# Where the row-maximum pieces of an attention stage stand between its score tiles: the second piece of a phase moved from the opening to the end

## The chip, the cores and the metric

The kernel runs on one core of a Trainium2 chip. The metric is device time in microseconds for one launch. Five engines work side by side and wait for each other by semaphores: TensorE (PE, with its weight loads shown apart as PEld), VectorE (DVE), ScalarE (ACT), GpSimd (POOL) and SyncE (SP, which issues the DMAs). Each takes its own instructions in the order in which the program lists them.

## The reference

An attention layer whose queries are pooled in pairs, followed by two MLP blocks that mix over the sequence and over the channels. Only the attention is touched here.

```python
batch, n_heads, seq, head_dim = (4, 8, 1152, 64)
q_pool = q.reshape(B, H, S // factor, factor, D).mean(axis=3)      # factor = 2: 576 queries
scores = scale * np.matmul(q_pool, k.transpose(0, 1, 3, 2))
scores = scores - np.max(scores, axis=-1, keepdims=True)
attn = np.exp(scores)
attn = attn / (np.sum(attn, axis=-1, keepdims=True) + 1e-09)
attn_out = np.matmul(attn, v)
# then _moe_ref (w_in, w_spatial, w_out) and _moe2_ref (U, V, w_ch1, w_ch2) on [4, 576, 512]
```

## The kernel before

The 32 heads are taken as 16 pairs, one head on partitions 0 to 63 and the other on 64 to 127. For a pair the scores are 576 queries by 1152 keys for each head; they are computed transposed (keys on partitions), since the second product needs them so. The row maxima that are subtracted must be known before the exponential, so they come from a separate pass with rounded operands, one pair ahead.

That pass is cut into 11 *pieces* a pair, 176 in all (`pieces`, `piece`). A piece is a few matmuls into a PSUM tile `r` and a maximum over that tile on DVE. There are three forms. The common one has two matmuls of 512 columns side by side (L169) and a reduce over 1024 columns (L191). The full-array one has two matmuls of 512 columns one after the other (L186, L187). The rest piece has four or six matmuls of 128 columns (L169, L199; L202), and when it is the second rest piece of a pair four small reduces follow it (L211, L214); every rest piece ends with L215. When all pieces of a pair are there, `to_rows` transposes the maxima on PE (L230, L237) and ACT copies them into a row (L240, L247).

The main loop runs over 108 *groups* `i` of four key chunks of 128, each chunk with 192 queries; 27 groups make four pairs. A group is two *score tiles* `s`: eight matmuls with q and k (L256), two that subtract the row of maxima (L272), then one exponential of 128x768 on ACT (L279). POOL adds the results up for the denominators (L297, L286, L300). After every odd group PE does the second product, `po` (L307), for the two groups before it, and, where a query third is complete, the sums (L321). So two groups, an even one and an odd one, make a *phase*: opening, two score tiles, a middle, two score tiles, an end, then a block of `po` matmuls. There are 54 phases.

Pieces may stand at the opening, in the middle and at the end. How many is set by `end`, which asks for a number of finished pieces that grows by 11 in 6.75 groups, and by `some(beside, lag)`, which puts one piece if fewer than `end - lag` are done. Before the change, an even group's opening puts one piece and then, with `lag=1`, possibly a second; the middle and the end put one each. The first five groups follow a table of their own (`FIRST`).

Score tiles, pieces and the transposed maxima all take their PSUM from one ring, `ps_s`, of three slots of two banks each. A new tile takes the slot that was given out three tiles earlier, and its first matmul waits until the last reader of that tile is through: the DVE reduce if it was a piece, the ACT exponential if it was a score tile.

Between the groups `also(i)` advances the preparation of the MLP weights: casts on ACT (L583, L584, L664), bit operations on DVE (L588, L590, L594), sums on POOL (L592, L669). The casts of the next pair's k and q (`round_k` L149, `round_q` L138 and L143) stand on ACT too, between the exponentials of two groups. On DVE the reciprocals of the sums (L329, two halves) and the product that makes an output tile (`out`, L335) stand among the reduces.

Of the kernel before, what the change touches and what calls it, by code (L numbers as in the profile page):

```python
# [30 lines left out]
FIRST = (11, 12, 15, 18, 21)  # L31
# [4 lines left out]
def attention(tc, idf, q, k, v, xs, rounded, also):  # L36
# [14 lines left out]
    NP, D, _, _, T = q.shape  # L51
    S = k.shape[3]
    HP = NP // len(xs)
    KC = S // 128
# [13 lines left out]
    with ExitStack() as ctx, ExitStack() as sco:  # L68
# [43 lines left out]
        def load_k(j, c0=0, c1=S):  # L112
            if "k" not in st[j]:
                st[j]["k"] = ld.tile([128, S], F32, tag="k", name="k", bufs=3)
            for e in range(2):
                nc.sync.dma_start(out=st[j]["k"][D * e:D * e + D, c0:c1], in_=k[j, :, e, c0:c1])

        def load_q(j, c0=0, c1=T):
            if "qraw" not in st[j]:
                st[j]["qraw"] = ld.tile([128, 2, T], F32, tag="qraw", name="qraw", bufs=2)  # L120
            for e in range(2):
                nc.sync.dma_start(out=st[j]["qraw"][D * e:D * e + D, :, c0:c1], in_=q[j, :, e, :, c0:c1])

        def load_v(j):
            t = st[j]["v"] = ld2.tile([128, 2, KC, D], F32, tag="v", name="v")
            nc.sync.dma_start(out=t, in_=v[j])
# [36 lines left out]
        upto = [sum(x[0] < u for x in pieces) for u in range(2 * NP + 1)]  # L163
        done = [0]
# [54 lines left out]
        def to_rows(*us):  # L219

            j = us[0] // 2
            if us[0] % 2 == 0:
                st[j]["top"] = ld.tile([128, T], F32R, tag="toprow", name="toprow")
            t = st[j]["top"]
            rs = ring("tr")
            cs = [2 * (u % 2) + c for u in us for c in range(2)]
            for c in cs:
                for i in range(2):
                    p = slice(64 * i, 64 * i + 64)
                    nc.tensor.matmul(  # L230
                        rs[:, i, 64 * c:64 * c + 64], tops[j % 2][p, c].rearrange("p e d -> p (e d)"), idr[p],
                        start=True, stop=True,
                    )
            if us[-1] % 2:
                for i in range(2):
                    p = slice(64 * i, 64 * i + 64)
                    nc.tensor.matmul(  # L237
                        rs[:, i, 256:320], tops[j % 2][p, 4].rearrange("p e d -> p (e d)"), idr[p], start=True, stop=True
                    )
            nc.scalar.copy(  # L240
                t[:, 128 * cs[0]:128 * cs[-1] + 128].rearrange("p (c i x) -> p i c x", i=2, x=64),
                rs[:, :, 64 * cs[0]:64 * cs[-1] + 64].rearrange("p i (c x) -> p i c x", x=64),
            )
            if us[-1] % 2:
                for i in range(2):
                    p = slice(64 * i, 64 * i + 64)
                    nc.scalar.copy(t[p, 512:T], rs[p, i, 256:320])  # L247

        def scores(pair):

            t = ps_s.tile([128, 2, 512], F32, tag="s", name="s")
            for x, (u, c) in enumerate(pair):
                s, q0 = st[u // 3], N * (u % 3)
                for e in range(2):
                    p = slice(D * e, D * e + D)
                    nc.tensor.matmul(  # L256
                        t[:, e, N * x:N * x + N], s["k"][p, 128 * c:128 * c + 128], s["q"][p, q0:q0 + N],
                        start=x == 0, stop=False,
                    )
            return t  # L260

        def less(pair, t):
            (u, _), (w, _) = pair
            for e in range(2):
                p = slice(D * e, D * e + D)
                top, q0 = st[u // 3]["top"], N * (u % 3)
                if u // 3 == w // 3:
                    if u == w:
                        m = top[p, q0:q0 + N].unsqueeze(1).broadcast_to([D, W, N])
                    else:  # L270
                        m = top[p, q0:q0 + W * N]
                    nc.tensor.matmul(t[:, e, 0:2 * N], first[p], m, start=False, stop=True)  # L272
                else:
                    for x, m in enumerate((top[p, q0:q0 + N], st[w // 3]["top"][p, 0:N])):
                        nc.tensor.matmul(t[:, e, N * x:N * x + N], first[p], m, start=False, stop=x == 1)

        def expo(pair, t):
            x = pt_p.tile([128, 2, W * N], F32, tag="pt", name="pt")
            nc.scalar.activation(x, t[:, :, 0:W * N], ACTF.Exp, scale=SC)  # L279
            for i, (u, c) in enumerate(pair):  # L280
                jobs[u]["p", c] = x[:, :, N * i:N * i + N]
            (u, c), (w, _) = pair
            jb = jobs[u]
            if u != w:
                a = jb["acc"][:, :, 0:N]
                nc.gpsimd.tensor_tensor(out=a, in0=a, in1=jb["p", c], op=ALU.add)  # L286
                return
            if u == NJ - 1 and c >= KC - 4:
                return

            if "t" not in jb:
                jb["t"] = x
            else:
                a = jb.get("acc")
                if a is None:
                    a = jb["acc"] = ld2.tile([128, 2, W * N], F32, tag="acc", name="acc")
                nc.gpsimd.tensor_tensor(out=a, in0=x, in1=jb["t"] if c < 4 else a, op=ALU.add)  # L297
                if u % 2 and c < 4:
                    a = a[:, :, 0:N]
                    nc.gpsimd.tensor_tensor(out=a, in0=a, in1=jb["p", 0], op=ALU.add)  # L300
# [86 lines left out]
        for i, group in enumerate(groups):  # L387
            if j + 1 < NP and at[j + 1] == i:
                j += 1
            r = i - at[j]  # L390
            if r == 0:
                if j + 2 < NP:
                    load_k(j + 2)
                    load_q(j + 2)
                if j + 1 < NP:
                    load_v(j + 1)

            end = min(upto[2] + -(-upto[2] * (4 * i + 8) // (3 * KC)), upto[2 * NP])
            if i < len(FIRST):
                end = min(end, FIRST[i])  # L400

            def some(beside=False, lag=0):
                if done[0] < end - lag:
                    piece(beside=beside)

            new = []
            if i == 2:
                new = [1]
            elif r == 0 and j:
                new = [2 * j, 2 * j + 1]  # L410
            for u in new:
                while done[0] < upto[u + 1]:
                    piece()
            if new:
                to_rows(*new)
            elif i % 2 == 0:
                some(True)
                if i > 3:
                    some(lag=1)
            for x in smalls.pop((i, 0), ()):  # L420
                x()
            ts = []
            for x in range(0, G, W):
                pair = group[x:x + W]
                ts.append((pair, scores(pair)))
                if i == 0 and x + W == G:
                    some()
                if i or x + W == G:
                    for y in ts:
                        less(*y)  # L430
                        expo(*y)
                    ts = []
            some(bool(i % 2))

            for _ in range(2 if i < 4 else 0):
                if done[0] < end:
                    piece(ps_s.tile([128, 2, 512], F32, tag="s", name="r1"))
            for x in smalls.pop((i, 1), ()):
                x()
            if i + 1 == len(groups):  # L440
                break
            if i == 0:
                round_q(1)
                round_k(1)
            if i % 2:
                for x in before:
                    pv(*x)
                before = []
                for u in sums_at.pop(i, ()):
                    sums(u)  # L450
            before = before + group
            also(i)
            if r == 2 and j + 2 < NP:
                pool_q(j + 2, nc.gpsimd)

            if r == 3 and j + 2 < NP:
                round_k(j + 2)
            if r == 4 and j + 2 < NP:
                round_q(j + 2)
# [926 lines left out]
```

## Time and profile before

| | |
|---|---|
| median of 3 runs | 1136.06 us (1135.66 to 1136.96) |
| the profiled execution | 1135.48 us, its span 1133.7 us |
| PE matmuls | 1107.6 us busy, 98% of the span |
| PE weight loads | 956.5 us, 84% |
| DVE, ACT, POOL | 589.3 us (52%), 446.4 us (39%), 540.8 us (48%) |
| attention stage | from 2 us to 484 us of the span, the rest is the two MLP blocks |

A matmul that is ready while the one before it still runs is shown as busy from its start, and the ends of matmuls are modelled. So the length of a piece of work on PE is best read from the start of its first matmul to the start of the next work's first matmul. Where a line of a timeline has "[0.26 <-DVE m L191]" at its end, the engine sat idle for that long, until the instruction named.

### The profile page before, as it was taken

The numbers are of one execution on the slowest core, as the hardware profiler recorded it, in microseconds if no ns is written. First come the engines' busy times: TensorE is split into PE (matmuls) and PEld (weight loads), VectorE is DVE, ScalarE is ACT, GpSimd is POOL, SyncE is SP. The second block draws the span as 40 slices with busy tenths as digits, with TensorE's granted clock in tenths as the row PEclk, the third lists the DMA queues.
The fourth block names the chain that finished last, engine by engine and source line by source line (L and its number), as shares of the span: only waits on it lengthen the run. The fifth ranks groups of instructions, "written<-read, shape, count | busy, mean of one in ns | idle before, by whom it ended". The sixth has DMA issues, their size and how long they took to land.

```text
span 1133.7 us, 20356 instructions
## 1 busy us (share of the span) xinstructions
PE 1107.6 (98%) x8406; PEld 956.5 (84%) x8406; DVE 589.3 (52%) x885; ACT 446.4 (39%) x824; POOL 540.8 (48%) x421
## 2 busy tenths in 40 slices
PE   8999999999999999999999999999999999999998
PEld 6777778788777878898988989899899999899897
DVE  6668878666878676254455553367612121211211
ACT  4555555465555555443343433355311111111110
POOL 4678789787798877624354545355500000000000
PEclk9999999999999999999999999999999999999999
DMA  6334333315425321013142506244202010010000
GB/s 167 104 76 113 104 93 94 86 56 134 113 62 142 87 57 36 9 59 103 65 131 84 164 28 191 91 138 129 86 1 84 1 57 1 1 57 1 29 1 28
DMA packets 44847, 86.65 MB, mean 76 GB/s; under 512 B 6353, under 2 KB 21329, under 8 KB 44754
## 3 DMA queue, kind: packets, MB, share of 16 engines
q1 hardware_dynamic: 44754, 85.35, 25.5%
q8 instruction: 66, 1.08, 0.4%
q14 instruction: 27, 0.22, 0.1%
HBM read 66.98 MB, written 17.83 MB: 75 GB/s over the span
## 4 chain that ended last, share of the span: by engine, by line
PE 54%; DVE 2%; ACT 1%; DMA 1%; POOL 0%; issue 0%; SPq 0%
PE ph L1230 17%; PE py L1244 17%; PE pg L981 5%; PE pu L963 4%; PE py L1012 4%; PE pv L828 3%; PE pV L1037 1%; PE pU L998 1%; PE pt L1222 1%; DMA cw<-st 1%; DVE bs L923 0%; DVE v L897 0%; DVE xt L485 0%; PE po L321 0%; DVE st L588 0%
## 5 line engine op out<-in xcount | busy, mean ns | idle before, releaser
L1244 PE MATMUL py<-w,h 128*128 128x512 f32 x864 | 217.1, 396 | 1.3 <-ACT h L1233 1.3
L1230 PE MATMUL ph<-ut,w 128*128 128x384 f32 x1152 | 218.0, 338 | 0.0
L1230 PEld LDWEIGHTS ph<-ut,w 128*128 128x128 f32 x1152 | 205.0, 188 | 8.4
L1234 DVE SCALAR_TENSOR_TENSOR h<-ph,h 128x384 fp32r<-128x384 f32 x96 | 53.5, 558 | 284.1 <-ACT h L1233 284.1
L279 ACT ACTIVATE pt<-s 128x768 f32<-128x768 f32 x216 | 172.0, 810 | 73.4 <-PE s L272 67.6
L191 DVE TENSOR_REDUCE m<-r 128x2 f32<-128x1024 f32 x128 | 154.6, 1221 | 82.8 <-PE r L169 82.6
L256 PE MATMUL s<-q,k 64*128 64x192 f32 x1728 | 184.9, 332 | 8.2 <-DVE m L191 7.0
L297 POOL TENSOR_TENSOR acc<-pt,acc 128x768 f32<-128x768 f32 x94 | 173.5, 1846 | 38.6 <-ACT pt L279 33.4
L1244 PEld LDWEIGHTS py<-w,h 128*128 128x128 f32 x864 | 160.0, 188 | 31.5 <-ACT h L1233 1.7
L1233 ACT ACTIVATE h<-ph 128x384 fp32r<-128x384 f32 x96 | 47.1, 491 | 310.6 <-PE ph L1230 309.0
L256 PEld LDWEIGHTS s<-q,k 64*128 64x128 f32 x1728 | 143.0, 187 | 27.3 <-DVE m L191 14.8
L307 PE MATMUL po<-pt,v 128*64 128x192 f32 x1728 | 154.4, 330 | 2.5 <-DVE x L335 2.5
L307 PEld LDWEIGHTS po<-pt,v 128*64 128x64 f32 x1728 | 118.5, 137 | 34.3 <-issue 15.1
L297 POOL TENSOR_TENSOR acc<-pt 128x768 f32<-128x768 f32 x48 | 88.4, 1841 | 40.2 <-ACT pt L279 40.2
L272 PE MATMUL s<-toprow,yh 64*128 64x384 f32 x416 | 98.7, 468 | 1.0 <-ACT toprow L240 1.0
L329 DVE RECIPROCAL sum<-sum 128x96 f32<-128x96 f32 x96 | 70.7, 741 | 28.9 <-ACT sum L325 28.9
L169 PE MATMUL r<-yh 64*128 64x512 f32 (+1 forms) x384 | 66.4, 385 | 3.9 <-DVE md L211 1.7
L325 ACT ACTIVATE sum<-po 128x192 f32<-128x192 f32 x48 | 15.9, 331 | 135.2 <-PE po L321 99.2
L981 PE MATMUL pg<-wst,vn 128*128 128x288 f32 x448 | 60.6, 296 | 0.8 <-DVE ut L987 0.8
L981 PEld LDWEIGHTS pg<-wst,vn 128*128 128x128 f32 x448 | 59.7, 188 | 1.3 <-DVE ut L987 1.3
L963 PEld LDWEIGHTS pu<-xt,wi 128*128 128x128 f32 x384 | 53.3, 188 | 2.0
L169 PEld LDWEIGHTS r<-yh 64*128 64x128 f32 x384 | 33.8, 185 | 24.5 <-issue 11.8
(150 smaller groups left out, 1353.6 us busy)
## 6 DMA issues: line engine op xcount, KB each, us to landing
raw<-in_moe_w_ch_dram SPq DMA_DIRECT2D x28, 512.0 KB, 3.7
v<-in_v_dram SPq DMA_DIRECT2D x16, 576.0 KB, 4.0
qraw<-in_q_dram SPq DMA_DIRECT2D x30, 288.0 KB, 5.6
k<-in_k_dram SPq DMA_DIRECT2D x30, 288.0 KB, 4.4
x<-x SPq DMA_DIRECT2D x48, 96.0 KB, 2.4
xn<-x SPq DMA_DIRECT2D x4, 1152.0 KB, 5.8
out_dram<-un SPq DMA_DIRECT2D x18, 256.0 KB, 2.1
raw<-in_moe_w_in_dram SPq DMA_DIRECT2D x8, 512.0 KB, 4.8
```

Source lines behind the costliest of these rows:

```text
L169: nc.tensor.matmul(o, s["qr"][p, q0:q0 + 128], s["kr"][p, k0:k0 + n], start=True, stop=True)
L191: nc.vector.tensor_reduce(out=m[:, c, :, k0 // PW], in_=r, axis=AX.X, op=ALU.max, negate=True)
L256: nc.tensor.matmul(t[:, e, N * x:N * x + N], s["k"][p, 128 * c:128 * c + 128], s["q"][p, q0:q0 + N], start=x == 0, stop=False,)
L272: nc.tensor.matmul(t[:, e, 0:2 * N], first[p], m, start=False, stop=True)
L279: nc.scalar.activation(x, t[:, :, 0:W * N], ACTF.Exp, scale=SC)
L297: nc.gpsimd.tensor_tensor(out=a, in0=x, in1=jb["t"] if c < 4 else a, op=ALU.add)
L307: nc.tensor.matmul(jb["o"][D * e:D * e + D, 0:N], st[u // 3]["v"][:, e, c], jb["p", c][:, e], start=c == 0, stop=c == KC - 1,)
L329: nc.vector.reciprocal(out=t, in_=t)
L963: nc.tensor.matmul(p[:, 0:HT], wi[0][:, a, k, 128 * m:128 * m + 128], xt[:, c, k, HT * h:HT * h + HT], start=i == 0, stop=i == 3 * KD - 1,)
L981: nc.tensor.matmul(p[:, 0:HT], vn[:, a, s, 128 * m:128 * m + 128], wst[:, c, s, sl], start=s == 0 and i == 0, stop=s == NT - 1 and i == 1,)
L1230: nc.tensor.matmul(p[:, 0:BT], w1s[m][:, a, k], ut[i][:, c, k], start=j == 0, stop=j == 3 * KD - 1)
L1244: nc.tensor.matmul(py[i][c], h[:, a, 128 * c:128 * c + 128], w2s[m][:, e], start=m == 0 and a + e == 0, stop=m == KM - 1 and a == 1,)
```

## The change

It changes when `some` is called and what `end` is. In every phase after the first five groups the opening holds one piece at most, the middle one (with `lag=1`), and the end one or two: two where one would leave fewer pieces done than `end` asks for. `end` of an even group is now that of the odd group behind it, so that a phase has one target.

```diff
-            end = min(upto[2] + -(-upto[2] * (4 * i + 8) // (3 * KC)), upto[2 * NP])
+            end = min(upto[2] + -(-upto[2] * (4 * (i | 1) + 8) // (3 * KC)), upto[2 * NP])
             if i < len(FIRST):
                 end = min(end, FIRST[i])
...
             elif i % 2 == 0:
                 some(True)
-                if i > 3:
-                    some(lag=1)
             for x in smalls.pop((i, 0), ()):
                 x()
...
-            some(bool(i % 2))
+            if i < len(FIRST):
+                some(bool(i % 2))
+            elif i % 2 == 0:
+                some(lag=1)
+            else:
+                some(done[0] + 1 >= end)
+                some(True)
```

The pieces themselves, their number, the score tiles, the `po` blocks and the work of `also` stay the same. Before, 20 phases open with two pieces and every phase ends with one at most. After, no phase opens with two, and 21 end with two.

On PE, in the phase of groups 10 and 11 (60.23 us in the trace of before), at its opening; `po` rows and L321 are the end of the phase before, `s` are the score tiles, `r` the pieces. Before:

```order
L321 MATMUL po<-acc,ones 64x192 x4
L169 MATMUL r<-yh 128x512 x4
L256 MATMUL s<-q,k 128x192 x4
L272 MATMUL s<-toprow,yh 128x384 x2
L256 MATMUL s<-q,k 128x192 x4
L272 MATMUL s<-toprow,yh 128x384 x2
L169 MATMUL r<-yh 128x512 x2
```

After:

```order
L321 MATMUL po<-acc,ones 64x192 x4
L169 MATMUL r<-yh 128x512 x2
L256 MATMUL s<-q,k 128x192 x4
L272 MATMUL s<-toprow,yh 128x384 x2
L256 MATMUL s<-q,k 128x192 x4
L272 MATMUL s<-toprow,yh 128x384 x2
L169 MATMUL r<-yh 128x512 x2
```

One of the two pieces at the opening is gone. At the end of the same phase PE has, before:

```order
L256 MATMUL s<-q,k 128x192 x4
L272 MATMUL s<-toprow,yh 128x384 x2
L256 MATMUL s<-q,k 128x192 x4
L272 MATMUL s<-toprow,yh 128x384 x2
L169 MATMUL r<-yh 128x512 x2
L307 MATMUL po<-pt,v 64x192 x16
L169 MATMUL r<-yh 128x128 x4
L199 MATMUL r<-yh 128x128 x2
```

After:

```order
L256 MATMUL s<-q,k 128x192 x4
L272 MATMUL s<-toprow,yh 128x384 x2
L256 MATMUL s<-q,k 128x192 x4
L272 MATMUL s<-toprow,yh 128x384 x2
L169 MATMUL r<-yh 128x512 x2
L169 MATMUL r<-yh 128x128 x4
L199 MATMUL r<-yh 128x128 x2
L307 MATMUL po<-pt,v 64x192 x16
L169 MATMUL r<-yh 128x512 x2
```

The rest piece stood behind the `po` block, as the next phase's opening, and now stands ahead of it, as the second piece of the end. On DVE, at the same end, the rows from the output product (`x`) to the middle of the next phase; `m` and `md` are the maxima, `st_113` a tile of the weight preparation. Before:

```order
L335 TENSOR_TENSOR x<-po,sum 128x192
L191 TENSOR_REDUCE m<-r 128x2
L588 TENSOR_SCALAR st_113<-st_113 128x512
L202 TENSOR_REDUCE m<-r 128x2x2
L211 TENSOR_REDUCE md<-r 64x1
L214 TENSOR_REDUCE yh<-md 64x1
L211 TENSOR_REDUCE md<-r 64x1
L214 TENSOR_REDUCE yh<-md 64x1
L215 TENSOR_REDUCE yh<-m 128x4
L191 TENSOR_REDUCE m<-r 128x2
L590 TENSOR_SCALAR st_113<-st_113 128x512
```

After (lines behind the change count four higher):

```order
L335 TENSOR_TENSOR x<-po,sum 128x192
L191 TENSOR_REDUCE m<-r 128x2
L202 TENSOR_REDUCE m<-r 128x2x2
L211 TENSOR_REDUCE md<-r 64x1
L214 TENSOR_REDUCE yh<-md 64x1
L211 TENSOR_REDUCE md<-r 64x1
L214 TENSOR_REDUCE yh<-md 64x1
L215 TENSOR_REDUCE yh<-m 128x4
L592 TENSOR_SCALAR st_113<-st_113 128x512
L191 TENSOR_REDUCE m<-r 128x2 x2
L594 TENSOR_SCALAR st_113<-st_113 128x512
```

The reduces of the second end piece now stand ahead of the weight preparation's row, and that row is later by them. ACT, POOL and SP have the same rows in the same order as before.

## Rows read from the trace of the kernel before

**Rows 1.** The page, part 1: busy time, share of the span and instructions by engine

```profile
PE 1107.6 (98%) x8406; PEld 956.5 (84%) x8406; DVE 589.3 (52%) x885; ACT 446.4 (39%) x824; POOL 540.8 (48%) x421
```

**Rows 2.** Waits of PE's weight loads, 34 to 448 us: total us, times, longest

```profile
PEld s L256 <- DVE m L191: 12.9, 21, 1.6
...
PEld r L169 <- DVE m L191: 6.0, 16, 0.7
PEld po L307 <- DVE x L335: 4.9, 7, 1.5
```

**Rows 3.** Timeline of PE, double opening: start us, us, instruction, idle

```profile
146.98 0.73 PE L169 MATMUL r<-yh 64*128 64x512 f32 x4
147.55 0.81 PE L256 MATMUL s<-q,k 64*128 64x192 f32 x8
...
148.80 0.92 PE L256 MATMUL s<-q,k 64*128 64x192 f32 x8 [0.26 <-DVE m L191]
...
149.94 0.50 PE L169 MATMUL r<-yh 64*128 64x512 f32 x2
...
151.93 0.39 PE L169 MATMUL r<-yh 64*128 64x512 f32 x2
```

**Rows 4.** Timeline of PE, a phase with a single opening

```profile
319.29 0.50 PE L169 MATMUL r<-yh 64*128 64x512 f32 x2
319.63 0.81 PE L256 MATMUL s<-q,k 64*128 64x192 f32 x8
...
321.28 0.39 PE L169 MATMUL r<-yh 64*128 64x512 f32 x2
...
323.34 0.39 PE L169 MATMUL r<-yh 64*128 64x512 f32 x2
323.66 2.82 PE L307 MATMUL po<-pt,v 128*64 128x192 f32 x32
```

**Rows 5.** Timeline of PE, a full-array opening (173.84) and the last double opening

```profile
173.84 0.73 PE L186 MATMUL r<-yh 128*128 128x512 f32 x2
...
176.26 0.40 PE L169 MATMUL r<-yh 64*128 64x512 f32 x2
...
430.98 0.67 PE L169 MATMUL r<-yh 64*128 64x512 f32 x6
...
433.74 0.40 PE L169 MATMUL r<-yh 64*128 64x512 f32 x2
```

**Rows 6.** Timeline of DVE, the first reduce at two openings

```profile
147.53 2.36 DVE L191 TENSOR_REDUCE m<-r 128x2 f32<-128x1024 f32 x2 [1.96 <-PE r L169]
...
301.15 0.69 DVE L202 TENSOR_REDUCE m<-r 128x4 f32<-128x512 f32 x1 [0.57 <-PE r L199]
```

**Rows 7.** Timeline, the phase at 60.23 us: PE's first row, then ACT

```profile
60.23 0.73 PE L169 MATMUL r<-yh 64*128 64x512 f32 x4
...
60.75 1.15 ACT L149 CAST yh<-k 128x1152 fp32r<-128x1152 f32 x1
...
63.27 0.81 ACT L279 ACTIVATE pt<-s 128x768 f32<-128x768 f32 x1 [0.56 <-PE s L272]
...
66.13 1.51 ACT L279 ACTIVATE pt<-s 128x768 f32<-128x768 f32 x2
```

**Rows 8.** Timeline of PE and ACT in the phases at 34.28, 388.21 and 422.88

```profile
34.28 0.73 PE L169 MATMUL r<-yh 64*128 64x512 f32 x4
...
39.04 1.51 ACT L279 ACTIVATE pt<-s 128x768 f32<-128x768 f32 x2
...
393.04 1.51 ACT L279 ACTIVATE pt<-s 128x768 f32<-128x768 f32 x2
...
393.46 0.42 PE L169 MATMUL r<-yh 64*128 64x512 f32 x2
...
426.69 1.64 ACT L279 ACTIVATE pt<-s 128x768 f32<-128x768 f32 x2 [0.43 <-PE s L272]
...
427.25 0.40 PE L169 MATMUL r<-yh 64*128 64x512 f32 x2
```

## The prediction, made before the changed kernel ran

> **What bounds the kernel now.** The page comes first: PE is busy for 98% of the span and every other engine for 52% or less [rows 1]. So the end is set by PE's program, and the change can gain only where PE stands still within it. The attention stage is the first 484 us; the page does not tell how much of that is standing still, because a matmul counts as busy while it waits behind another. The waits view of the weight loads is next. From 34 to 448 us, the stretch that has nearly all pieces, loads for score tiles waited 12.9 us in 21 waits for a piece's reduce on DVE, and loads for pieces 6.0 us in 16 [rows 2]. 20 phases open with two pieces, so these look like one or two waits per double opening. The timeline of PE shows it, read from start to start. With two pieces the opening and two score tiles take from 146.98 to 149.94, 2.96 us [rows 3]; with one piece they take from 319.29 to 321.28, 1.99 us [rows 4]. The second piece itself needs 0.23 of the difference: the pieces take 0.57 (146.98 to 147.55) against 0.34 (319.29 to 319.63). The other 0.74 is waiting.
>
> The cause is the ring of three slots. The second score tile asks for the slot of the opening's first piece, the middle piece for that of the second, and DVE makes the two reduces one after the other, 2.36 us for both [rows 6]. The idle of 0.26 that the row at 148.80 carries names DVE [rows 3].
>
> **What the change removes.** At 14 of the 20 double openings both pieces are common ones; the first is at 34.28 [rows 8]. Each loses 0.97 us, and the piece that left costs its 0.23 at an end. After a double opening the way from the middle piece to the end piece is a little shorter, 1.99 us (149.94 to 151.93) against 2.06 (321.28 to 323.34) [rows 3, 4], since the exponentials have caught up by then; I take off 0.07. That leaves 0.67, times 14 is 9.4 us. The other six have a rest piece in the pair. The last takes 2.76 (430.98 to 433.74), and a full-array piece alone, which stands there in some phases afterwards, takes 2.42 (173.84 to 176.26) [rows 5]; the other pieces only change places. I take 0.4 for each of the six, between the 0.34 of these two rows and the 0.67 above: 2.4 us. Sum: 11.8 us.
>
> In up to six of these phases ACT has the cast of k (1.15 us) ahead of the first exponential [rows 7]. It ends at 61.90, so that exponential, 0.81 long, ends at 62.7, while with one piece at the opening the third score tile asks for that slot at 60.23 + 1.99 + 0.34 = 62.56 (0.34 from a piece to the tile behind it, as at the opening). I take off 0.2 for each at most, 1.0 in all.
>
> **What the change adds.** 21 ends now have two pieces. Their matmuls are counted. The wait is not: the second end piece asks for the slot of the phase's third score tile, so it needs that tile's exponential, and no piece before stood at that place. Queued behind it on PE are the `po` block, the sums, and the whole next phase. It asks 0.23 us after the first end piece. In 14 of the 21 the exponential is just through: at 426.69 it starts, 0.81 later it ends, at 427.50, and the piece would ask at 427.25 + 0.23 = 427.48 [rows 7, 8]. I take 0.06 each, 0.8 in all. In seven ACT is behind, because casts of q or weight work stand between the second and the third exponential. The worst is the phase at 60.23. There, the second exponential waited 0.56 for PE; it can now follow the first after 0.70 (1.51 for two, 0.81 for one), at 62.60 instead of 63.27, and everything up to the third, which started at 66.13, moves up by that 0.67 [rows 7]. The third then ends at 66.27. The piece asks at 60.23 + 1.99 + 2.06 + 0.23 = 64.51, and 0.2 later for the delay just named: a wait of 1.6 us. The first of the seven in the trace gives 0.5 in the same way (39.04 moves up by 0.8 and ends at 39.05, asked for at 34.28 + 4.28 = 38.56), the last 0.2 (393.85 against 393.69) [rows 8]. All seven together give 5.0. So this term is 5.8 us, with 0 and 13 as its ends: nothing if the exponentials move up more than I let them, and 13 if the 14 that are just in time become late by the 0.6 of an average late one, as PE gets ahead.
>
> I take the two other effects at nothing. On DVE the second reduce of an end falls under the `po` block, whose first part alone takes 2.8 us on PE [rows 4]. The reduce needs 1.2 (half of 2.36), and in front of the next opening's reduce DVE sat idle for 1.96 in a usual phase and for 0.57 in the tightest of the 21 [rows 6]. If that cover were gone, the next middle piece would wait, 1.1 us once for the tightest. On the other side, one reduce fewer stands ahead of the output product, for which `po` waited 4.9 us in 7 waits [rows 2]; some of that may go, 2 us at most as I judge it, since few of the seven follow a double opening. The weight preparation on DVE is pushed back by one or two reduces in 21 phases; nobody on PE waits for it in this stage. SP and POOL keep their order, and POOL has room in the phase (541 us busy in all).
>
> **The sum.** 11.8 - 1.0 - 5.8 = 5.0 us. The profiled execution took 1135.48 us and its span is 1133.7, so 1135.5 - 5.0 = 1130.5. The median of the three runs is 0.6 above the profiled execution: 1131.1, and I give 1131.
>
> **The rivals.** *The wait only changes its owner.* Three slots serve the same number of tiles, and a piece that no longer waits at the opening waits at the end, for ACT in place of DVE. For it: the ring is not larger, and in seven ends ACT is already behind. Against it: behind the second end piece comes a `po` block which uses no slot of the ring, so its reduce has some 3 us, where at the opening it had under 2. It gives no change where the mean wait of the 21 reaches 10.8 / 21 = 0.51 us; mine is 0.28. Time: 1136. The Trainium skill speaks for this rival: Perfetto Trace Analysis, Optimization Strategy, says that the same gap repeating on the engine that should be saturated can mean that SBUF or PSUM is too small for the next tile. By that rule the order is not the cure, and the trace agrees as to the ring.
>
> *All of the opening's gain arrives.* ACT has its exponentials earlier than I let it, and the second end piece finds its slot free. For it: 14 of the 21 lie within 0.1 us already. Against it: the casts between the exponentials stay where they are. Time: 1136.1 - 10.8 = 1125.3.
>
> *ACT falls behind everywhere.* It is one mechanism at one place: the second end piece waits for the third exponential. PE's phases get shorter by 0.67 us, ACT's work in them doesn't, so the 14 that are just in time become late too. At 0.6 us for each of them the term is 5.8 + 8 = 14 and the time 1136.1 + 3 = 1139. It decides from a mean wait of 0.62 on (13.1 / 21), where the loss passes 2.3 us. Against it: before most exponentials ACT waits for PE and not the other way round, as at 63.27 and 426.69 [rows 7, 8].
>
> That the change does not do what it says is excluded by the order on PE: 21 double ends, no double opening.
>
> **How the numbers follow.** The forecast (a gain of 2.3 to 9 us) has 0.58, the full gain 0.16, the change of owner 0.17, ACT falling behind 0.09. 0.2% is 2.3 us, about what a measurement of this kernel can tell from no change. So faster 0.74, same 0.17, slower 0.09. The range that should hold 8 times in 10 takes in the full gain at one end and the change of owner at the other: 1125 to 1136.5.
>
> **What would show it.** In the trace of the changed kernel the way from an opening to its middle piece is 2.0 us in every phase without a transpose, and the waits of score tiles' loads for L191 fall from 12.9 to under 4 us. New rows "PE or PEld r <- ACT pt L279" appear, some 5 to 6 us in all, longest about 1.6, in the phase of groups 10 and 11. In the two kinds of phase where nothing is doubled, lengths stay. The forecast is wrong if those new waits are under 2 or over 10 us, if score tiles still wait for DVE, which would mean that the end's reduces don't fit under `po`, or if the time after the attention stage, some 650 us, changes.

## The result, and the profile after

| | before | after |
|---|---|---|
| median, on one chip with each other (4 runs each) | 1136.12 us (1135.66 to 1136.96) | 1126.07 us (1125.42 to 1126.45) |
| ratio, with its 95% interval | | 0.9912 (0.9899 to 0.9924) |
| span of the profiled execution | 1133.7 us | 1124.1 us |
| first piece of groups 4/5 to first score tile of groups 102/103 | 34.28 to 455.44: 421.2 us | 34.29 to 445.87: 411.6 us |
| from there to the end of the span | 678.3 us | 678.2 us |

The change gains 10.0 us where 5.0 were forecast. All of it lies between groups 4 and 102. That stretch is called *the stage* below; it is read from PE's timeline, and its length is used to compare kernels, because the head in front of it varies by up to 3.6 us between traces. It is longest where the granted clock falls in it: in the run with casts and pooling earlier it is 0.5 (1.2 GHz) from 12.8 to 19.6 us and the stage begins at 37.38, in the changed kernel it is 1.0 throughout and the stage begins at 34.29.

The first part of the page of the changed kernel answers to [rows 1]:

```profile
PE 1103.5 (98%) x8406; PEld 956.2 (85%) x8406; DVE 584.5 (52%) x885; ACT 446.1 (40%) x824; POOL 541.7 (48%) x421
```

The shares hardly show the change. PE has the same 8406 instructions and is 98% busy as before. In absolute numbers its idle time fell from 26.1 us (1133.7 less 1107.6) to 20.6 and its busy time by 4.1 us with the same instructions, so a part of the waiting had counted as busy. DVE, with the same 885 instructions, is 4.8 us less busy, although none of its work went; that is taken up again below.

The waits of PE's weight loads in the changed kernel, from 34 to 440 us (total us, times, longest), answer to [rows 2]:

```profile
...
PEld r L169 <- ACT pt L279: 9.8, 17, 1.8
PEld s L256 <- ACT pt L279: 8.9, 33, 0.4
PEld po L307 <- DVE x L335: 2.4, 5, 0.9
...
PEld r L169 <- DVE m L191: 1.7, 3, 0.9
...
PEld r L186 <- ACT pt L279: 1.4, 4, 0.5
...
PEld s L256 <- DVE m L191: 0.9, 2, 0.6
```

Score tiles waited for DVE's reduce for 12.9 us and now wait for 0.9. Pieces wait for ACT's exponential instead, in 17 waits, and in four more where the second piece is a full-array one (L186); all but one of them are at the new double ends. So the owner of the wait did change, but the new waits (11.2 us) are smaller than those for DVE were (12.9, and 6.0 of the pieces). Score tiles' waits for an earlier exponential rose from 6.0 to 8.9.

PE's timeline of the phase of groups 30 and 31 in the changed kernel answers to [rows 3]:

```profile
145.57 0.51 PE L169 MATMUL r<-yh 64*128 64x512 f32 x2
...
147.56 0.41 PE L169 MATMUL r<-yh 64*128 64x512 f32 x2
...
149.63 0.39 PE L169 MATMUL r<-yh 64*128 64x512 f32 x2
```

From the opening to the middle it takes 1.99 us (145.57 to 147.56), where it took 2.96; the middle takes 2.07. This phase has no second piece at its end either and is 0.89 us shorter.

The worst of the new ends is the one that the prediction named, in the phase of groups 10 and 11. First PE, then ACT, both of the changed kernel:

```profile
64.21 0.39 PE L169 MATMUL r<-yh 64*128 64x512 f32 x2
66.01 0.44 PE L169 MATMUL r<-yh 64*128 64x128 f32 x4 [1.41 <-ACT pt L279]
...
66.49 2.82 PE L307 MATMUL po<-pt,v 128*64 128x192 f32 x32
```

```profile
61.59 1.50 ACT L279 ACTIVATE pt<-s 128x768 f32<-128x768 f32 x2
62.99 0.66 ACT L587 ACTIVATE st<-raw 128x512 f32<-128x512 f32 x1
...
64.12 0.61 ACT L138 CAST yh<-q 128x512 fp32r<-128x512 f32 x1
...
65.15 1.51 ACT L279 ACTIVATE pt<-s 128x768 f32<-128x768 f32 x2
```

ACT makes two exponentials, two weight operations and the casts of q before the third exponential starts at 65.15. It is through 0.81 later, at 65.96, and the second end piece, which could have started 0.23 behind 64.21, starts at 66.01: 1.6 us late. The `po` block behind it is late by the same.

### The profile page after: what moved, and what is told of

Read it like the earlier page. It is cut to its first block, busy times and chain, and to the rows that moved or that the text cites. A ratio compares the mean times of both kernels' runs of the same rounds, so it can differ in the third digit from the quotient of the medians.

```text
span 1124.1 us, 20357 instructions
## 1 busy us (share of the span) xinstructions
PE 1103.5 (98%) x8406; PEld 956.2 (85%) x8406; DVE 584.5 (52%) x885; ACT 446.1 (40%) x824; POOL 541.7 (48%) x421
## 4 chain that ended last, share of the span: by engine, by line
PE 53%; DVE 2%; POOL 1%; ACT 1%; DMA 1%; issue 0%; SPq 0%; POOLq 0%
PE ph L1234 18%; PE py L1248 17%; PE pu L967 5%; PE pg L985 4%; PE py L1016 4%; PE pv L832 2%; PE pV L1041 1%; PE pU L1002 1%; PE pt L1226 1%; POOL gt L489 1%; DVE bs L927 1%; DMA cw<-st 1%; POOL st L656 0%; DVE v L901 0%; DVE xt L489 0%
## 5 line engine op out<-in xcount | busy, mean ns | idle before, releaser
L307 PEld LDWEIGHTS po<-pt,v 128*64 128x64 f32 x1728 | 118.7, 137 | 30.7 <-issue 13.6
L329 DVE RECIPROCAL sum<-sum 128x96 f32<-128x96 f32 x96 | 70.8, 742 | 31.4 <-ACT sum L325 31.4
L169 PE MATMUL r<-yh 64*128 64x512 f32 (+1 forms) x384 | 68.1, 383 | 6.7 <-ACT pt L279 5.0
L325 ACT ACTIVATE sum<-po 128x192 f32<-128x192 f32 x48 | 15.9, 332 | 140.7 <-PE po L321 102.4
L169 PEld LDWEIGHTS r<-yh 64*128 64x128 f32 x384 | 34.9, 184 | 27.0 <-ACT pt L279 13.0
```

The lines of the kernel that those rows point to most:

```text
L169: nc.tensor.matmul(o, s["qr"][p, q0:q0 + 128], s["kr"][p, k0:k0 + n], start=True, stop=True)
L307: nc.tensor.matmul(jb["o"][D * e:D * e + D, 0:N], st[u // 3]["v"][:, e, c], jb["p", c][:, e], start=c == 0, stop=c == KC - 1,)
L329: nc.vector.reciprocal(out=t, in_=t)
```

## The experiments

Each kernel is compared with the kernel before on the same chip, whose median was 1135.8 to 1136.1 us.

| kernel | time, us | ratio to before (95%) | stage, us |
|---|---|---|---|
| before | 1136.1 | | 421.2 |
| after | 1126.1 | 0.9899 to 0.9924 | 411.6 |
| before, target by phase only | 1144.8 | 1.0061 to 1.0091 | 429.8 |
| after, old target | 1147.9 | 1.0086 to 1.012 | 433.4 |
| after, second piece in the middle | 1137.2 | 1.0001 to 1.0019 | 423.0 |
| before, weight preparation behind the attention | 1197.5 | one run | 412.3 |
| after, weight preparation behind the attention | 1186.0 | one run | 403.4 |
| before, weight preparation one group later | 1151.4 | 1.0124 to 1.0154 | 436.7 |
| after, weight preparation one group later | 1140.6 | 1.003 to 1.0066 | 425.2 |
| after, casts and POOL's pooling earlier | 1125.2 | 0.9893 to 0.9922 | 410.1 |
| after, casts alone earlier | 1123.9 | 0.9876 to 0.991 | 409.0 |
| after, run again beside the last | 1126.9 | 0.9904 to 0.9931 | 411.5 |

### Each half of the change alone

The change has two halves: the target `end` by phase, and the places of the second piece. The first experiment makes only the first half, in the kernel before:

```diff
-            end = min(upto[2] + -(-upto[2] * (4 * i + 8) // (3 * KC)), upto[2 * NP])
+            end = min(upto[2] + -(-upto[2] * (4 * (i | 1) + 8) // (3 * KC)), upto[2 * NP])
```

> The kernel before with one line of the change alone: the target of an even group is that of the odd group behind it. The slots stay as before, so 41 phases open with two pieces in place of 20, and their ends are empty. Theory (the place of the second piece decides): every further double opening costs the 0.66 us that was read from phases which lost one, 21 x 0.66 = 14, so 1150 us. Rival (the earlier target is itself what gains, since pieces come sooner): below 1136, about 1130.

The stage became 8.7 us longer and the time 8.6 us. With the higher target at the even group, 41 phases open with two pieces instead of 20, and many ends are empty. So the direction is the theory's, and its rival, which had the time fall, is out. The size is smaller: 8.7 / 21 = 0.41 us for each added double opening, where a common one had cost 0.67. From phase to phase, the openings became 17.8 us longer, 0.85 for each added one, and the ends, 20 of which lost their only piece, 8.0 us shorter, 0.40 each. The double openings are not alike: 13 of the 41 pair a common piece with a rest piece of four matmuls and take 2.56 to 2.76 us, 14 hold a full-array piece or a rest piece of six and take 3.18 to 3.64, and two common ones take 2.95. The target alone is no gain at all.

The second makes only the other half, by taking the target back in the changed kernel:

```diff
-            end = min(upto[2] + -(-upto[2] * (4 * (i | 1) + 8) // (3 * KC)), upto[2 * NP])
+            end = min(upto[2] + -(-upto[2] * (4 * i + 8) // (3 * KC)), upto[2 * NP])
```

> The changed kernel with the old target for even groups. No phase opens with two pieces, but 48 ends have two in place of 21, and their middles are empty. Theory: no double opening, so the gain of the openings stays (about 10 us in openings and none back); the 27 further double ends each pay the wait of a usual end, 0.1 to 0.2 us, and those in which ACT is behind 0.6 to 1.7; an empty middle saves the 0.1 that the third score tile waits behind a middle piece. Sum about +2 to +6: 1128 to 1132. Rival (the target decides): back at 1136.

This expectation was wrong by 15.9 us or more. The old target asks for less at the middle of a phase, so in 29 of the 49 phases the middle now has no piece, and 48 ends are double. From phase to phase the middles became 10.8 us shorter and the ends 32.2 longer. PE and then ACT of this kernel in the phase of groups 10 and 11:

```profile
60.28 0.50 PE L169 MATMUL r<-yh 64*128 64x512 f32 x2
...
62.27 0.81 PE L256 MATMUL s<-q,k 64*128 64x192 f32 x8
...
63.92 0.39 PE L169 MATMUL r<-yh 64*128 64x512 f32 x2
66.29 0.50 PE L169 MATMUL r<-yh 64*128 64x512 f32 x2 [1.98 <-ACT pt L279]
```

```profile
65.42 1.51 ACT L279 ACTIVATE pt<-s 128x768 f32<-128x768 f32 x2
```

The opening is 1.99 us as in the changed kernel, and the way through the middle is 1.65 (62.27 to 63.92) instead of some 2.1. But PE comes to the end earlier while ACT does not: the second end piece waits 2.1 us (66.29 less 63.92, less the piece's 0.23). It is not only the late phase that pays. The phase of groups 16 and 17, whose end takes 0.32 in the changed kernel, ends here in 2.18, and the loads of pieces (L169) wait 31.4 us for exponentials from 34 to 455 us, against 9.8. A piece in the middle keeps PE busy while ACT works off the first two exponentials; taken from there and put at the end, it costs what it weighs and the wait besides. This is the rival in which the wait only changes its owner, and it wins as soon as the middle is empty. The target by phase is what keeps a piece in every middle.

### The second piece in the middle instead of at the end

```diff
             elif i % 2 == 0:
+                some(lag=2)
                 some(lag=1)
             else:
-                some(done[0] + 1 >= end)
                 some(True)
```

> The changed kernel with the second piece in the middle of the phase in place of its end (20 double middles, no double opening, no double end). Theory (a second piece is cheap only where the PO block follows it): behind a double middle come two score tiles and the end piece, which ask for slots within 2 us; the third score tile waits for the second exponential, and the end piece for the second reduce. About 1 us each, 20 us, less the 8 us of end waits that go: 1138 us. Rival (any place but the opening will do): 1126 or less, since the end waits go.

1137.2 us, near the theory's 1138, and the rival's 1126 is out. PE in the phase of groups 10 and 11, from the middle to the end:

```profile
65.70 0.95 PE L169 MATMUL r<-yh 64*128 64x512 f32 x4
66.85 0.92 PE L256 MATMUL s<-q,k 64*128 64x192 f32 x8 [0.20 <-ACT pt L279]
...
68.61 0.38 PE L169 MATMUL r<-yh 64*128 64x128 f32 x4
```

The way from the middle to the end is 2.91 us here; with one piece it is 2.06 [rows 4]. So a double middle costs 0.85, of which 0.23 is the piece, about as much as the double opening of before (0.97). Against the same phases of the changed kernel 18 of the 20 double middles cost 0.87 on the mean. Two pieces side by side cost a wait wherever two score tiles follow them, and only the end, where a `po` block follows that takes no slot of the ring, is cheap: at the 14 ends where ACT is on time it costs 0.35 on the mean (below).

Not all of the 11.4 us by which this stage is longer than the changed kernel's are of that kind. The edit leaves the end of groups 5 with one piece, so a rest piece stands ahead of the transposes at the opening of groups 6: PE waits 1.72 us there for DVE, and the opening takes 5.20 us instead of 2.34. Behind that wait, from 46.3 to 49.7 us, the granted clock is 0.5 (1.2 GHz), and once more from 162.3 to 165.7, behind a wait of 0.88. Without the 2.9 us of that one opening the time would, as an estimate, be 1134.3: still 8 us above the changed kernel's, but no longer above that of the kernel before. That the place behind which the slots are not needed is better than the middle is shown by this run; that the middle is as bad as the opening was is not shown by its time, but by its phases.

### Was the surplus of 5 us luck in the place of the weight preparation?

After the result two accounts were open for the gain beyond the forecast. By the first, DVE had been late at a few places of the old order because of the weight preparation, and by accident was not so in the new one; then the gain would shrink without that work, or where it stands elsewhere. By the second the openings themselves give 10 us. Four runs: in both kernels the preparation was moved behind the attention stage (nothing of it is left out, but it then lies on the path, so the whole time is 60 us longer), and in both it was started one group later.

```diff
-        if i == WEIGHTS:
-            w.load(units, raws)
-        if i >= WEIGHTS + 2:
-            w.tick()
...
+    w.load(units, raws)
     w.end()
```

> The kernel before without the weight preparation during the attention stage: its casts, bit operations, sums and loads all come behind the attention, so the whole time is longer by the preparation (some tens of us), and only the attention stage is compared, from the trace (start of the last four groups' phases). Theory A (5 of the 10 us gained were waits of PE for DVE in phases where weight operations on DVE ran long beside POOL's additions): without them those waits go in this kernel too, the stage is some 5 to 8 us shorter than before's, and the changed kernel without weight work gains only 5 to 7 us on it. Theory B (the gain is all of the pieces' places): the changed kernel gains 10 us here as well.

> The changed kernel without the weight preparation during the attention stage (it comes behind it, so the whole time is longer). Theory A: the stage ends 5 to 7 us earlier than in the kernel before without weight work. Theory B: 10 us earlier.

Only the stage can be compared: 412.3 us against 403.4, at a granted clock of 1.0 in both. The change gains 8.9 us there without any weight work, against 9.6 with it. Openings give 19.0, middles and ends cost 10.1, and `po` blocks do not change. So the second account is the nearer one, but not for its reason alone. With the weight work, ends wait some 4 us more (7.6 us at the double ends of the changed kernel beyond the pieces themselves, 3.7 in this run), and the places where DVE was late give about as much back; the two happen to cancel.

```diff
-WEIGHTS = 8
+WEIGHTS = 9
```

> The kernel before with the weight preparation started one group later, so that each of its operations stands in a group of the other kind (odd for even). Theory A (waits for DVE's weight operations depend on where they fall): the time moves by 1 to 6 us, either way, and the difference to the changed kernel shifted alike is not 10 but that of the openings and ends alone, 4 to 8. Theory B: 1136, and the pair differs by 10.

> The changed kernel with the weight preparation started one group later. ACT's weight operations now stand behind the sums and ahead of the next opening's exponentials, no longer between the second and third exponential. Theory A: the end waits of the phases of groups 18, 60 and 74 (0.9, 0.35 and 0.8 us) fall to 0.2, and the waits for DVE change: 1122 to 1128. Theory B: 1126.

The gain of the change is 10.9 us here (1151.4 less 1140.6), so the first account falls as far as the sum goes: the gain did not shrink. But its parts did hang on where the preparation stands. Openings give 19.1 us of the stage as before, ends cost 8.7, middles now cost 5.1 and `po` blocks give 6.3; that the sum is again near 10 is in part chance. 2.7 of the 6.3 are one `po` block of the shifted kernel before, in the phase of groups 68, where PE stood 2.85 us for the product L335 and the granted clock was 0.5 (1.2 GHz) from 328.3 to 332.0 us, just behind that wait.

One part of the last expectation came true: with ACT's weight operations moved, the ends at groups 18, 60 and 74 fall from 1.45, 0.91 and 1.26 us to 0.74, 0.72 and 0.65, so they had been late for those operations. Both expected times failed: a shift by one group costs either kernel some 15 us, which nobody had expected. In the kernel before, 13.6 of the 15.6 us by which its stage grew are `po` blocks. The waits of the weight loads in the shifted kernel before, from 34 to 448 us, have a new first row:

```profile
PEld po L307 <- DVE x L335: 16.7, 10, 3.2
```

It was 4.9 in 7 waits [rows 2]. One of the ten, first on PE and then on DVE of the same kernel:

```profile
182.72 1.52 PE L307 MATMUL po<-pt,v 128*64 128x192 f32 x16
186.61 1.52 PE L307 MATMUL po<-pt,v 128*64 128x192 f32 x16 [2.37 <-DVE x L335]
```

```profile
182.58 1.50 DVE L588 TENSOR_SCALAR pair<-pair 128x512 f32<-128x512 f32 x1
184.01 2.29 DVE L594 SCALAR_TENSOR_TENSOR st<-raw,st 128x512 int32<-128x512 int32 x1
186.21 0.34 DVE L335 TENSOR_TENSOR x<-po,sum 128x192 f32<-128x192 f32 x1
```

Two weight operations of 3.8 us together now stand ahead of the product for which the second half of the `po` block waits. It is the same work one group later, and it costs more than the whole change gained.

### The late ends: ACT's casts out of the way

If the seven late ends are due to casts and weight operations between ACT's second and third exponential, they should become shorter when the casts go elsewhere. The place is the odd group, ahead of the second product, where ACT waits for PE anyway.

```diff
             if i % 2:
+                for n, cast in ((2, round_k), (3, round_q)):
+                    if n <= r <= n + 1 and j + 2 < NP:
+                        cast(j + 2)
                 for x in before:
                     pv(*x)
...
-            if r == 2 and j + 2 < NP:
+            if r == 1 and j + 2 < NP:
                 pool_q(j + 2, nc.gpsimd)
-            if r == 3 and j + 2 < NP:
-                round_k(j + 2)
-            if r == 4 and j + 2 < NP:
-                round_q(j + 2)
```

> The changed kernel with the casts of the next pair's k and q moved on ACT: always in an odd group, ahead of the PO block and of the sums, so that none stands between the second and the third exponential of a phase, and none behind the sums (the sum of q's two halves on POOL one group earlier). Theory (the large end waits are those of ACT's casts): the ends of the phases of groups 4, 10 and 64, which wait 0.7, 1.7 and 1.3 us, fall to about 0.2, 3 us in all; 1123 us. Rival (the end piece waits because the ring is short, whatever ACT does): no change, 1126.

The ends behaved: the one at groups 10 went from 2.29 to 1.51 us, at 64 from 1.86 to 0.96, at 4 from 1.29 to 0.79. The sum did not: 1125.2 us, not told apart from the changed kernel, and a stage that is shorter by 1.5 us instead of 3. Two openings, in the phases of groups 16 and 36, went from 1.99 to 2.9. PE and DVE of this kernel in the first of them:

```profile
88.01 0.50 PE L169 MATMUL r<-yh 64*128 64x512 f32 x2
...
90.92 0.50 PE L169 MATMUL r<-yh 64*128 64x512 f32 x2 [0.76 <-DVE m L191]
```

```profile
85.86 1.65 DVE L591 TENSOR_SCALAR st<-st 128x512 f32<-128x512 f32 x1
87.43 2.30 DVE L597 SCALAR_TENSOR_TENSOR st<-raw,st 128x512 int32<-128x512 int32 x1
89.66 1.21 DVE L191 TENSOR_REDUCE m<-r 128x2 f32<-128x1024 f32 x1
```

DVE came to the opening's reduce at 89.66, since two weight operations had run until then. The first of them had run beside POOL's pooling of q, which the edit had also put one group earlier. The next kernel leaves POOL where it was and moves only the casts:

```diff
-            if r == 1 and j + 2 < NP:
+            if r == 2 and j + 2 < NP:
                 pool_q(j + 2, nc.gpsimd)
```

> The changed kernel with ACT's casts of k and q moved to the odd groups, ahead of the second product, and nothing else (POOL's pooling of q stays where the changed kernel has it). Theory (the losses of the casts-and-pooling run came from POOL's earlier pooling, beside which DVE's weight operations stretched): the ends at groups 10 and 64 take 1.5 and 1.0 us instead of 2.29 and 1.86, that at group 4 0.8 instead of 1.29, and the openings of the phases at groups 16 and 36 are back at 1.99; the stage from group 4 to group 102 takes 408 to 409 us instead of 411.6, the time is 1123 us. Rival (the ends' gain is used up by whatever follows them, wherever the pooling stands): 1125.3 to 1126.1, the stage 410 to 411.5.

1123.9 us (1123.78 to 1123.96 in 4 runs); the changed kernel, run beside it, took 1126.9 (1125.79 to 1127.62 in 5). The stage is 409.0 us, the openings at 16 and 36 are back at 1.99, and the gains at the ends stay. On DVE of this kernel the same two weight operations:

```profile
83.27 0.42 DVE L591 TENSOR_SCALAR st<-st 128x512 f32<-128x512 f32 x1
83.60 2.31 DVE L597 SCALAR_TENSOR_TENSOR st<-raw,st 128x512 int32<-128x512 int32 x1
85.97 1.23 DVE L191 TENSOR_REDUCE m<-r 128x2 f32<-128x1024 f32 x1
```

The first of them takes 0.42 where it took 1.65, and the opening's reduce is in time. The late end at groups 10, first on PE and then on ACT of this kernel:

```profile
64.36 0.39 PE L169 MATMUL r<-yh 64*128 64x512 f32 x2
65.37 0.44 PE L169 MATMUL r<-yh 64*128 64x128 f32 x4 [0.62 <-ACT pt L279]
```

```profile
59.07 0.62 ACT L138 CAST yh<-q 128x512 fp32r<-128x512 f32 x1 [0.91 <-POOL q L132]
...
64.53 1.50 ACT L279 ACTIVATE pt<-s 128x768 f32<-128x768 f32 x2
```

The cast of q now runs at 59.07, under the `po` block, and the piece waits 0.8 us instead of 1.6. What is left stands behind the two weight operations that are still there; no run moved both them and the casts. This kernel is faster than both kernels of the case.

> The changed kernel itself, on the same chip as the run with the casts moved, so that the two can be compared: 1126.1 us, the stage from group 4 to group 102 411.6 us within 0.5.

The run of the changed kernel gave 1126.9 us and a stage of 411.5, as expected.

## Why the prediction came out as it did

The direction and the mechanism were right and the measured 1126.1 lies in the range of 1125 to 1136.5, but near its fast end. The gain was mis-sized by half. The terms of the sum, measured by the phases of the stage, from start to start on PE:

| term | forecast, us | measured, us |
|---|---|---|
| openings and middles, with the 0.23 a piece at the end | +11.8, less 1.0 for the cast of k | +15.1 |
| waits at the 21 double ends | -5.8 | -7.6 |
| `po` blocks (waits for the product L335) | 0 | +2.1 |
| sum | +5.0 | +9.6 |

The measured column is worked out from the 49 phases of the stage: openings 20.3 us shorter, middles 0.4 longer, ends 12.5 longer (of which 4.8 is the 21 pieces at 0.23 and nearly all the rest, 7.6, waiting at the 21 double ends), `po` blocks 2.1 shorter; 20.3 less 0.4 less 4.8 is the 15.1.

**The 14 common openings.** Right. The opening fell to 1.99 us in all but one of them, and the common loss was the 0.97 of [rows 3, 4]. That score tiles' waits for the reduce would fall from 12.9 to under 4 us was also right: 0.9. The sign that every opening without a transpose takes 2.0 did not hold where a full-array piece opens (2.42, as in [rows 5]).

**The six mixed openings.** This term was mis-sized: 0.4 each was taken, and they gave 4.5 us together from phase start to phase start, 0.75 each. The estimate compared a common piece with a rest piece (2.76) against a full-array piece alone [rows 5], but in two of the six, at groups 42 and 96, the opening now holds a rest piece alone and takes 1.98. The sixth, at groups 46, held a rest piece of six with a common one and took 3.64 where it takes 1.99 now; its rows in the trace of before had that length, and the prediction did not price them.

**The cast of k ahead of the first exponential.** Too much: 1.0 us was taken off, and beyond the 0.07 that was already counted the middles of those phases became longer by 0.15 at most (2.21 at groups 10), some 0.2 in all. Without the weight preparation the same middles take 2.21 in all five phases where 1.99 stood, so there the term comes out near its size; why it does not beside the preparation stays open.

**The waits at the ends.** The step held in kind and in its largest number: 1.6 us was forecast for the phase at 60.23, and 1.6 came. The late ends cost 5.9 us against 5.0, of which the prediction worked out three of seven. The 14 on time cost 0.12 each on the mean against 0.06, so 1.7 against 0.8: with two common pieces such an end takes 0.73 where it took 0.33. The rival in which ACT falls behind everywhere did not come: it asked for 0.6 at each of these. The size of the new rows was not met: 5 to 6 us were forecast, with 10 as the limit, and they have 9.8 us at common and rest pieces and 1.4 more at full-array ones (L186).

**DVE's side effects, taken at nothing.** This is the step that failed. The prediction said that nobody on PE waits for the weight preparation in this stage; but without that work the stage of the kernel before is 8.9 us shorter (421.2 against 412.3). The step allowed up to 2 us for the product L335, and 2.1 came: the row fell from 4.9 us in 7 waits to 2.4 in 5. It allowed nothing for the openings, and another 2 us came there, because DVE's weight operations ran into them less. The phase of groups 24 and 25 before, on PE and then on DVE:

```profile
122.82 0.92 PE L256 MATMUL s<-q,k 64*128 64x192 f32 x8 [1.27 <-DVE m L191]
...
123.95 0.50 PE L169 MATMUL r<-yh 64*128 64x512 f32 x2
```

```profile
117.84 1.56 DVE L588 TENSOR_SCALAR pair<-pair 128x512 f32<-128x512 f32 x1
119.32 2.32 DVE L594 SCALAR_TENSOR_TENSOR pair<-raw,pair 128x512 int32<-128x512 int32 x1
121.56 2.34 DVE L191 TENSOR_REDUCE m<-r 128x2 f32<-128x1024 f32 x2
```

The opening at 119.99 had its first piece ready early, but DVE was on weight work until 121.6. It took 3.96 us to the middle, a full microsecond more than a usual double opening, and was counted with 0.97. After, on DVE:

```profile
117.85 0.89 DVE L592 TENSOR_SCALAR pair<-pair 128x512 f32<-128x512 f32 x1
118.67 2.31 DVE L598 SCALAR_TENSOR_TENSOR pair<-raw,pair 128x512 int32<-128x512 int32 x1
120.89 1.21 DVE L191 TENSOR_REDUCE m<-r 128x2 f32<-128x1024 f32 x1
```

DVE is through 0.7 earlier, only one reduce stands there, and the opening takes 2.29: 1.67 gained instead of 0.97, so 0.7 beyond the forecast. What stood beside the first of these rows on POOL differs, before and then after:

```profile
117.26 1.85 POOL L297 TENSOR_TENSOR acc<-pt 128x768 f32<-128x768 f32 x1
```

```profile
117.05 1.40 POOL L132 TENSOR_TENSOR q<-qraw 128x576 f32<-128x576 f32 x1
```

Each time DVE's row ends 0.3 us behind POOL's, at 119.40 and 118.74 (more on this in the last section). In the same way the opening at groups 32 gave 0.9 and that at 72 0.35, neither of which is a double opening. One opening went the other way, at groups 80 from 2.00 to 2.79, of which the middle behind it gave 0.61 back. With the 2.1 of the `po` blocks that makes some 4 us. That they come from the weight preparation is shown by the kernel before without it in the stage: its openings at 24, 32 and 72 take 2.95, 2.11 and 1.99 us, where they took 3.96, 3.58 and 2.34 with it, and no `po` block waits. The longer waits at the ends, for ACT's part of the same work, take about as much.

**The rivals.** That the whole of the opening's gain arrives and the ends cost nothing would have given 1125.3, close to the 1126.1 measured, but it is not what happened: the waits at the ends cost 7.6 us. The time came near that figure by luck, through terms that nobody had put in. That the wait only changes its owner did not come here, but it did with an empty middle (1147.9). Phases that keep one common piece at each place keep their 7.8 us, as forecast, and so do the 678 us behind the stage.

## What to carry to other kernels

When several producers share a ring of few slots, put the extra one ahead of a stretch of work that takes no slot, and check both neighbours: here the same piece cost 0.97 us ahead of score tiles at the opening, 0.87 in the middle, and 0.35 ahead of the `po` block where ACT is on time. Do not empty one place to fill another, since a place that looks like padding may be the time in which another engine catches up (an empty middle cost 22 us against the changed kernel). And size a term instance by instance where a filler job on the same engine moves: three openings (groups 24, 32 and 46) were off by 0.7 to 1.1 us each, and their own rows in the trace of before showed that they were not of the usual kind.

## What the runs showed of the hardware

A weight operation on DVE has no fixed duration beside POOL's work; it tends to end just behind the POOL operation beside it. Two weight rows of the kernel before and the same two of the changed kernel, on DVE at the same place:

```profile
100.37 2.05 DVE L588 TENSOR_SCALAR pair<-pair 128x512 f32<-128x512 f32 x1
102.35 2.30 DVE L594 SCALAR_TENSOR_TENSOR st<-raw,st 128x512 int32<-128x512 int32 x1
```

```profile
101.50 0.93 DVE L592 TENSOR_SCALAR pair<-pair 128x512 f32<-128x512 f32 x1
102.36 2.30 DVE L598 SCALAR_TENSOR_TENSOR st<-raw,st 128x512 int32<-128x512 int32 x1
```

In the changed kernel one more reduce stands ahead of the first row, which starts 1.13 us later, takes 1.12 less, and ends at the same 102.43. POOL's row is the same in both, here of the kernel before:

```profile
100.32 3.77 POOL L297 TENSOR_TENSOR acc<-pt,acc 128x768 f32<-128x768 f32 x2
```

The first of the two additions ends near 102.2, half of 3.77 behind 100.32, and the weight row ends just behind it, whenever it began. In the trace of before, 15 of the 16 rows of L588 begin beside a POOL operation, and 11 of these end 0.28 or 0.29 us behind its end. A row that begins beside none takes 0.42 (67.05 us in the trace of before, 68.26 after).

So the second reduce at that end cost DVE nothing. DVE's 4.8 us less of busy time come from the weight operations, and not all in one direction: summed over the stage, L588 takes 7.8 us less after the change, L590 2.6 less and L594 4.5 more (numbers of the kernel before). In the kernel with the casts alone moved, L591 began at 83.27, at the seam between two additions, and took 0.42; in the one with the pooling earlier it began 0.05 behind POOL's pooling and took 1.65. POOL of the two kernels:

```profile
81.44 3.92 POOL L297 TENSOR_TENSOR acc<-pt,acc 128x768 f32<-128x768 f32 x2
```

```profile
85.81 1.41 POOL L132 TENSOR_TENSOR q<-qraw 128x576 f32<-128x576 f32 x1
```

The Trainium skill, SBUF — State Buffer, "SBUF: two separate sides", says that a VectorE operation in a 2-port perf mode or with two inputs in SBUF and a GpSimd operation take a shared pair of ports as an exclusive lock, held by whichever starts first for the whole instruction. The rows of L588 and L591 agree with that: where POOL's operation began first, most of them end 0.3 us behind it. No run here took POOL's additions away to show it by itself.
